# A thresholded attention with a gated MLP behind it: the MLP's products of a batch gathered in one round of the written order, and PSUM evictions that VectorE or ScalarE may take

## The chip, the cores and the metric

The kernel runs on one core of a Trainium2 chip. Its time is the device time of one execution, in microseconds (us). TensorE (PE), VectorE (DVE), ScalarE (ACT), GpSimd (POOL) and SyncE (SP, which issues most DMAs here) each take their instructions in order.

## What is computed

q, k and v are 8 batches x 8 heads x 576 positions x 64, in float32. Attention keeps only the scores within tau of the row's maximum; its output goes through a gated MLP whose gate mixes the 576 positions:

```python
scores = 0.125 * q @ k^T                             # per batch b and head h, 576 x 576
keep   = scores >= max(scores, -1) - tau             # tau = 0.02
attn   = where(keep, exp(scores - max), 0);  attn /= sum(attn) + 1e-9
x      = (attn @ v), heads side by side              # 8 x 576 x 512
h      = relu(x @ w_in);  u, v = h[..., :512], h[..., 512:]
v_n    = (v - mean(v)) / sqrt(var(v) + 1e-6)         # over the last axis
v_s    = w_spatial @ v_n + b_spatial[:, None]        # over the 576 positions
out    = (u * v_s) @ w_out                           # 8 x 576 x 512, float32
```

The kernel's v (attention) and the MLP's v half are different things; below, "values" are the second.

## The kernel before

**Steps and rounds.** Two heads of one batch form a pair; there are 32 pairs, four to a batch. A step is 128 query rows of both heads of a pair, 144 steps in all: four steps to a pair, and after each second pair one more step for the last 64 rows of two pairs together. One batch is 18 steps, and a round of the loop (`it`, 0 to 7) runs the 18 steps of batch `it` with other batches' MLP work between them.

**The written order.** `ORDER` has four strings of tokens: rounds 0, 1, 2, and one for rounds 3 to 7. A token is a name and a lag: `v2:1` in round 5 is work v2 of batch 4. `run_token` skips what is done already, and what belongs to no batch. A capital letter is mostly TensorE's part, the small one the eviction of its PSUM bank. The tokens are emitted in that order, so this is also the order in each engine's queue. The names:

- S, G, Y: score products of a step (`scores`, L661), a POOL instruction that passes the bank on (`turn_bank`), and the remaining score products, which wait for it. M: the row maximum on VectorE (negm, `top`, L688). E, F: one ScalarE activation for each head (e, L702 or L705).
- A step is of one of two kinds, by `on_act` and the list `ON_ACT`. In the first, B adds tau on VectorE (L694), E and F are Prelu with a slope of 1e30 below the threshold (L702), and Z takes the exponential on ScalarE (L722). In the second, E and F take the exponential (L705), and W compares and multiplies on VectorE (L717).
- T, TR: DMA transposes of p and pr to pT and ptr on SP; RP, rp: the latter on TensorE with a copy out of PSUM (L470). P, R and p, r: product with v (L358, L363), and division by the sum on VectorE (L370, L372) into xn. X, XR: DMA transposes of xn into xT; XP, xp: the same on TensorE (L444, L451).
- QA, QB, QR and qa, qb, qr: transposes of q and k on TensorE, with copies out of PSUM into qkT (L316, L318, L333); kd, sq, sv: reshaping copies on POOL; L: loads on SP.
- v0 to v4: value products (L511; v4 is L496, and holds beside it the last 64 output rows of the batch before, L499); ev: relu with a sum (L519); n, k, N: mean on POOL, squares on ScalarE (L533), norm on POOL into vn (L539 to L543). u0 to u4 and eu: the u half, relu into uT (L558, L563; L573, L575). s0 to s4 and es: spatial products (L588, L593) and the gate on VectorE (gT, L602, L605). o0 to o3 and eo: output products (L617) and a copy (L625); OUT: the output's DMA.
- Ci, Co, Cs, Cb with a small s behind them: load and reshaping of w_in, w_out, w_spatial and the bias; WS, ws: transposes of w_spatial and their copies (L481, L485).

All products but the scores go through two PSUM banks (`bank`, tile f), so a product waits for the eviction of the product two before it. The scores have two rings of three banks (s).

**The end.** After the loop W and T of the last step follow (`LAST`). Then there are six more banks (tile t), and `left` lists which v, u, s and o of batches 5 and 6 the rounds have not done; `run` does them, with the last products of attention (pv, pv_rest, x_pe) between. `last_gmlp` is the MLP of batch 7: value products (L754), norms (L777 to L788), spatial products (L796, L803), output products (L828, L817).

## Time and profile before

| what | us |
| --- | --- |
| median of 13 runs | 453.04 (451.59 to 456.6) |
| the profiled execution, its own time | 455.22 |
| its span, first to last instruction | 453.3 |
| first negm of rounds 0 to 7 | 8.83, 56.24, 107.96, 157.51, 209.29, 260.82, 312.33, 363.84 |
| last negm ends | 412.3 |

TensorE's mean granted clock is 0.987 of full speed. A window is the stretch between two such starts; busy time is what an engine spent on instructions in it, and a wait is an engine's idle time put down to the instruction that ended it. An instruction's time runs to its end, while the next on that engine can start a little before: times of groups are durations, and the start of one to the start of the next is what a queue takes when nothing waits.

### The profile page before, as it was taken

How to read it: one execution, taken by the hardware profiler on the slowest of the kernel's cores; microseconds unless marked ns; L12 is line 12 of the kernel's file. 1: busy time of each engine (PE TensorE's matmuls, PEld its weight loads, DVE VectorE, ACT ScalarE, POOL GpSimd, SP SyncE). 2: the span in 40 equal slices, each digit the busy share in tenths (PEclk: the TensorE clock that was granted, in tenths of full speed). 3: DMA queues.
4: the chain of work that ended last, by engine and by line, in shares of the span. 5: the costliest groups of instructions: out<-in, count | busy, mean ns of one | idle time of the engine just before them, and what ended most of it. 6: DMA issues, size and time to landing. Idle time of an engine off the chain costs nothing.

```text
span 453.3 us, 12711 instructions
## 1 busy us (share of the span) xinstructions
PE 417.6 (92%) x4981; PEld 263.6 (58%) x5035; DVE 387.0 (85%) x556; ACT 400.7 (88%) x697; POOL 184.4 (41%) x403
## 2 busy tenths in 40 slices
PE   7678778888999999999999999999999999999995
PEld 4455555565656566656666656656665656656542
DVE  5788699978999988999799987999799987997573
ACT  3998899899999999999999999999999999999241
POOL 1352347744366625242444516243344507136021
PEclk9998899989999999999999999999999999999999
DMA  7999998779999999999999999998989997779423
GB/s 224 236 253 203 220 189 221 158 163 180 205 207 226 201 210 205 186 222 207 226 177 226 187 223 211 167 258 200 224 180 193 211 229 148 133 153 176 133 104 106
DMA packets 222845, 88.15 MB, mean 194 GB/s; under 512 B 193601, under 2 KB 218305, under 8 KB 222785
## 3 DMA queue, kind: packets, MB, share of 16 engines
q1 hardware_dynamic: 222128, 86.45, 91.6%
q8 instruction: 40, 0.66, 0.6%
q0 software_dynamic: 160, 0.52, 0.3%
q10 hardware_dynamic: 496, 0.36, 0.2%
q14 instruction: 21, 0.16, 0.1%
HBM read 32.79 MB, written 9.44 MB: 93 GB/s over the span
## 4 chain that ended last, share of the span: by engine, by line
PE 39%; DVE 31%; ACT 16%; issue 6%; DMA 5%; POOL 1%; POOLq 0%; DVEq 0%; ACTq 0%
PE s L661 15%; DVE negm L688 15%; DVE p L717 10%; ACT e L702 6%; ACT e L705 4%; DMA pT<-p 3%; PE f L558 3%; PE f L311 2%; DVE xn L372 2%; PE f L617 2%; PE f L363 2%; PE f L588 2%; ACT vrel L519 1%; PE f L496 1%; DVE gT L602 1%
## 5 line engine op out<-in xcount | busy, mean ns | idle before, releaser
L688 DVE TENSOR_REDUCE negm<-s 128x2 f32<-128x1152 f32 x144 | 194.3, 1352 | 35.7 <-PE s L661 33.6
L661 PE MATMUL s<-qkT 64*64 64x160 f32 (+1 forms) x2304 | 177.0, 421 | 15.5 <-ACT e L705 7.5
L661 PEld LDWEIGHTS s<-qkT 64*64 64x64 f32 x2304 | 107.7, 134 | 68.5 <-ACT e L705 19.2
L705 ACT ACTIVATE e<-s,negm 128x576 f32<-128x576 f32 x144 | 103.4, 752 | 10.7 <-DVE negm L688 8.4
L702 ACT ACTIVATE e<-s,negm 128x576 f32<-128x576 f32 x144 | 102.1, 750 | 6.1 <-DVE negm L694 4.4
L717 DVE SCALAR_TENSOR_TENSOR p<-e,ctau 128x1152 bf16<-128x1152 f32 x72 | 105.1, 1461 | 2.6 <-ACT e L705 2.5
L722 ACT ACTIVATE p<-e 128x1152 bf16<-128x1152 f32 x56 | 65.5, 1174 | 0.2
L323 POOL COPY qkT<-qkT 64x64 f32<-64x64 f32 x32 | 12.2, 382 | 82.9 <-ACT qkT L333 61.7
L363 PE MATMUL f<-v,pT 128*128 128x65 bf16 x992 | 45.1, 195 | 0.0
L363 PEld LDWEIGHTS <-pT 128*128 128x128 bf16 x1024 | 42.2, 98 | 3.7 <-issue 0.8
L214 POOL CAST v<-vl 128x512 bf16<-128x512 f32 x32 | 20.3, 635 | 57.4 <-PE s L661 56.8
L372 DVE TENSOR_TENSOR xn<-f,r 128x256 bf16<-128x256 f32 (+1 forms) x92 | 35.0, 380 | 3.0 <-DVE r L370 0.2
L588 PE MATMUL f<-wsT,vn 128*128 128x512 bf16 x118 | 30.8, 380 | 1.5 <-DVE xn L372 0.9
L543 POOL TENSOR_SCALAR vn<-vrel,rs,nm 128x512 bf16<-128x512 f32 (+1 forms) x35 | 28.1, 802 | 3.8
L527 POOL TENSOR_SCALAR nmean<-sm 128x1 f32<-128x1 f32 (+1 forms) x35 | 11.6, 332 | 42.4 <-PE s L661 32.8
L558 PE MATMUL f<-xT,w_in 128*128 128x512 bf16 x94 | 27.8, 380 | 1.0
L511 PE MATMUL f<-w_in,xT 128*128 128x512 bf16 x93 | 27.7, 381 | 1.0
L358 PE MATMUL f<-v,pT 128*128 128x130 bf16 x124 | 27.4, 221 | 0.8 <-ACT uT L573 0.4
L533 ACT ACTIVATE sq<-vrel,nmean 128x512 bf16<-128x512 f32 (+1 forms) x35 | 25.5, 728 | 1.6 <-POOL nmean L527 1.0
L191 POOL COPY qn<-ql 128x512 f32<-128x512 f32 x31 | 20.5, 660 | 9.7 <-PE s L661 6.4
L617 PE MATMUL f<-w_o,gT 128*128 128x512 bf16 x83 | 22.4, 380 | 0.3
L519 ACT ACTIVATE vrel<-f 128x512 f32<-128x512 f32 (+1 forms) x34 | 20.3, 596 | 2.7 <-PE f L499 2.6
(160 smaller groups left out, 582.3 us busy)
## 6 DMA issues: line engine op xcount, KB each, us to landing
vl<-in_v_dram SPq DMA_DIRECT2D x16, 512.0 KB, 4.6
ql<-in_q_dram SPq DMA_DIRECT2D x15, 512.0 KB, 5.1
kl<-in_k_dram SPq DMA_DIRECT2D x15, 512.0 KB, 5.2
out_dram<-oo SPq DMA_DIRECT2D x10, 512.0 KB, 4.8
uT<-in_moe_w_in_dram SPq DMA_DIRECT2D x3, 512.0 KB, 5.3
uT<-in_moe_w_spatial_dram SPq DMA_DIRECT2D x2, 576.0 KB, 4.9
vx<-in_v_dram SPq DMA_DIRECT2D x16, 64.0 KB, 3.7
pT<-p SPq DMA_TRANSPOSE x64, 5.7
```

The lines of the kernel that those rows point to most:

```text
L363: nc.tensor.matmul(out=t[:, at + 65 * h:at + 65 * h + 65], lhsT=pt[:, 5 * h + j, :], rhs=vt[:, 6 * h + j, :], start=False, stop=(h == 1 an ...
L372: nc.vector.tensor_tensor(out=dst, in0=o[ps, g0:g1, 0:64], in1=r[ps, g0:g1].unsqueeze(2).broadcast_to([ps.stop - ps.start, g1 - g0, 64]), ...
L543: nc.gpsimd.tensor_scalar(out=vn_ring[b % 2][:n, c, :], in0=hold["vrel"][:n], scalar1=rs[:n], scalar2=nm[:n], op0=ALU.mult, op1=ALU.add)
L558: nc.tensor.matmul(out=t, lhsT=w_in[:, m, f * P:(f + 1) * P], rhs=x_of(b, m, slice(0, 512)), start=(m == 0), stop=(m == 3))
L588: nc.tensor.matmul(out=t, lhsT=vn[:, c, f * P:(f + 1) * P], rhs=wsT[:, c, 0:512], start=(c == 0), stop=(c == 4))
L617: nc.tensor.matmul(out=t[:n], lhsT=gs[b][:, f, c * P:c * P + n], rhs=w_o[:, f, :], start=(f == 0), stop=(f == 3))
L661: made.append(nc.tensor.matmul(out=s_ring[g % 2][halves[k], at[h] + lo:at[h] + hi], lhsT=qks[n][halves[h], 0, m:m + 64], rhs=qks[n][halves ...
L688: nc.vector.tensor_reduce(out=nm, in_=view(s_ring[g % 2], at[0], [[at[1] - at[0], 2], [1, S]]), axis=AX.X, op=ALU.max, negate=True)
L702: nc.scalar.activation(out=e, in_=s, func=ACT.Prelu, bias=bias_, scale=scale if steps[g][1] == 4 else 1.0, alpha=1e30)
L705: nc.scalar.activation(out=e, in_=s, func=ACT.Exp, bias=bias_)
L717: nc.vector.scalar_tensor_tensor(out=numerators(g), in0=ef, scalar=ctau, in1=ef, op0=ALU.is_ge, op1=ALU.mult)
L722: nc.scalar.activation(out=numerators(g), in_=e_ring[g % 3].rearrange("p h s -> p (h s)"), func=ACT.Exp)
```

## The change

The four strings of `ORDER` and the list `ON_ACT` are written anew, and a token may begin with d: its eviction then runs on VectorE instead of ScalarE, through a new helper `evict`. The products, their tiles and their number stay.

| | before | after |
| --- | --- | --- |
| steps with the exponential in Z, rounds 0, 1, 2, 3 to 7 | 11, 8, 8, 9 | 13, 11, 9, 10 |
| evictions marked d | none | 9, 14, 5, 7 |
| v, u, s, o in round 1 | v0 to v3, u0 of batch 0 | v0 to v4, u0 to u4, s0 of batch 0 |
| in round 2 | v4, u1 to u4, s0 to s4 of batch 0; v0 to v3, u0 of batch 1 | s1 to s4, o0 to o3 of batch 0; v0 to v4, u0 to u4, s0 of batch 1 |
| in each later round r | v4, u1 to u4, s0 to s4 of batch r-2; v0 to v3, u0 of r-1; o0 to o3 of r-3 | s1 to s4, o0 to o3 of batch r-2; v0 to v4, u0 to u4, s0 of r-1 |
| left for the end | v4, u1 to u4, s0 to s4, o0 to o3 of batch 6; o0 to o3 of batch 5 | s1 to s4, o0 to o3 of batch 6 |
| reshaping of w_spatial | round 1 | Cs1, Cs2, Cs0 and Css2, Css4, Css3 in round 0, Css0, Css1 in round 1 |
| its transposes WS, ws | three in round 1, two in round 2 | five in round 1 |
| reshaping of w_out | round 2 | three of four in round 1, one in round 2 |
| loads of batch 1's k and q (L1:-1, L0:-1) | in round 0 after step 4 and step 7 | first in round 0, and after step 0 |

The last string, `ON_ACT`, and the helper with its users (the first three strings are left out):

```diff
 (
-    "S0:0 G0:0 Y0:0 QA1:0 M0:0 v4:2 qa1:0 S1:0 ev4:2 B0:0 W17:1 G1:0 Y1:0 u1:2 F0:0 M1:0 E0:0 R1:1 T31:1 "
-    "eu1:2 S2:0 r1:1 Z0:0 G2:0 Y2:0 QB1:0 M2:0 E1:0 o0:3 qb1:0 F1:0 u2:2 B2:0 E2:0 W1:0 S3:0 eo0:3 G3:0 "
-    "eu2:2 Y3:0 F2:0 QR1:0 M3:0 o1:3 L3:-1 qr1:0 Z2:0 kd1:0 L0:-1 sq2:0 P30:1 B3:0 eo1:3 S4:0 p30:1 n4:2 "
-    "E3:0 G4:0 sq3:0 Y4:0 F3:0 QA2:0 M4:0 T00:0 P31:1 qa2:0 Z3:0 S5:0 p31:1 G5:0 sv1:0 B4:0 Y5:0 E4:0 "
-    "QR2:0 M5:0 u3:2 qr2:0 F4:0 kd2:0 L6:-1 QB2:0 eu3:2 X1:1 S6:0 F5:0 G6:0 sv2:0 Y6:0 qb2:0 o2:3 M6:0 "
-    "E5:0 sv0:0 k4:2 T01:0 S7:0 W5:0 E6:0 G7:0 N4:2 Y7:0 eo2:3 o3:3 F6:0 M7:0 P00:0 Z4:0 S8:0 p00:0 L1:-1 "
-    "G8:0 eo3:3 W6:0 Y8:0 OUT4:3 E7:0 u4:2 v0:1 eu4:2 M8:0 F7:0 QA3:0 ev0:1 S9:0 T10:0 qa3:0 B8:0 W7:0 "
-    "G9:0 F8:0 Y9:0 QR3:0 s1:2 E8:0 M9:0 qr3:0 Z8:0 P01:0 L5:-1 B9:0 S10:0 es1:2 E9:0 G10:0 TR0:0 sv3:0 "
-    "p01:0 Y10:0 F9:0 QB3:0 M10:0 S11:0 qb3:0 G11:0 n0:1 kd3:0 Y11:0 F10:0 T11:0 v1:1 M11:0 E10:0 s0:2 "
-    "ev1:1 B11:0 W10:0 Z9:0 S12:0 G12:0 n1:1 E11:0 Y12:0 es0:2 L2:-1 sq0:-1 R0:0 F11:0 M12:0 L4:-1 P10:0 "
-    "k1:1 S13:0 r0:0 E12:0 G13:0 N1:1 Y13:0 p10:0 F12:0 v2:1 T20:0 M13:0 Z11:0 QA0:-1 sq1:-1 ev2:1 S14:0 "
-    "B13:0 W12:0 G14:0 qa0:-1 Y14:0 F13:0 s2:2 OUT1:3 M14:0 E13:0 P11:0 L8:-1 Z13:0 es2:2 S15:0 G15:0 "
-    "p11:0 k0:1 n2:1 Y15:0 QR0:-1 M15:0 k2:1 s3:2 N0:1 T21:0 qr0:-1 F14:0 v3:1 es3:2 E14:0 B15:0 kd0:-1 "
-    "E15:0 QB0:-1 W14:0 S16:0 ev3:1 G16:0 qb0:-1 Y16:0 n3:1 N2:1 F15:0 P20:0 M16:0 TR1:0 k3:1 s4:2 Z15:0 "
-    "S17:0 es4:2 p20:0 X0:0 G17:0 N3:1 Y17:0 F16:0 u0:1 M17:0 E16:0 P21:0 T30:0 eu0:1 W16:0 E17:0 F17:0 "
-    "p21:0 L9:-1 OUT3:3 L7:-1 ")]
+    "S0:0 G0:0 Y0:0 QA1:0 M0:0 QR1:0 qa1:0 S1:0 qr1:0 G1:0 B0:0 Y1:0 W17:1 E0:0 QB1:0 F0:0 s1:2 M1:0 "
+    "qb1:0 Z0:0 S2:0 T31:1 G2:0 es1:2 Y2:0 B1:0 s3:2 M2:0 F1:0 E1:0 R1:1 sv1:0 es3:2 S3:0 B2:0 r1:1 F2:0 "
+    "L3:-1 G3:0 kd1:0 Y3:0 sq2:0 E2:0 L1:-1 s2:2 M3:0 Z1:0 sq3:0 S4:0 B3:0 es2:2 F3:0 G4:0 Y4:0 T00:0 "
+    "E3:0 o0:2 M4:0 Z2:0 P30:1 deo0:2 S5:0 B4:0 p30:1 G5:0 E4:0 Y5:0 F4:0 QA2:0 M5:0 L0:-1 P31:1 Z3:0 "
+    "S6:0 p31:1 qa2:0 G6:0 sv2:0 Y6:0 X1:1 F5:0 o1:2 M6:0 sv3:0 E5:0 o2:2 eo1:2 W5:0 T01:0 E6:0 QB2:0 "
+    "F6:0 S7:0 eo2:2 G7:0 W6:0 Y7:0 qb2:0 S8:0 Z4:0 G8:0 sv0:0 Y8:0 M7:0 L7:-1 QR2:0 s4:2 qr2:0 L4:-1 "
+    "kd2:0 v0:1 es4:2 E7:0 M8:0 v1:1 F7:0 ev0:1 W7:0 S9:0 T10:0 ev1:1 G9:0 Y9:0 F8:0 n1:1 QR3:0 o3:2 "
+    "dqr3:0 M9:0 E8:0 v2:1 k1:1 W8:0 eo3:2 S10:0 L6:-1 ev2:1 G10:0 n0:1 TR0:0 Y10:0 E9:0 P01:0 n2:1 M10:0 "
+    "kd3:0 sq0:-1 F9:0 P00:0 k0:1 S11:0 B10:0 p01:0 F10:0 T11:0 G11:0 N0:1 p00:0 Y11:0 E10:0 QB3:0 M11:0 "
+    "v3:1 qb3:0 Z10:0 W9:0 QA3:0 S12:0 OUT3:2 ev3:1 G12:0 dqa3:0 Y12:0 E11:0 OUT1:2 v4:1 M12:0 F11:0 u1:1 "
+    "ev4:1 W11:0 T20:0 S13:0 eu1:1 n4:1 G13:0 Y13:0 B12:0 N1:1 E12:0 QR0:-1 M13:0 R0:0 qr0:-1 F12:0 "
+    "QA0:-1 k2:1 S14:0 B13:0 r0:0 G14:0 F13:0 N2:1 Y14:0 dqa0:-1 E13:0 P10:0 L8:-1 M14:0 Z12:0 P11:0 "
+    "OUT4:2 n3:1 L2:-1 S15:0 p10:0 k4:1 G15:0 kd0:-1 p11:0 Y15:0 F14:0 N4:1 u4:1 M15:0 T21:0 P20:0 eu4:1 "
+    "E14:0 u0:1 p20:0 k3:1 B15:0 W14:0 u2:1 F15:0 E15:0 S16:0 deu0:1 Z13:0 G16:0 N3:1 Y16:0 deu2:1 u3:1 "
+    "M16:0 Z15:0 X0:0 QB0:-1 sq1:-1 S17:0 eu3:1 B16:0 dqb0:-1 G17:0 E16:0 TR1:0 Y17:0 s0:1 F16:0 M17:0 "
+    "Z16:0 T30:0 P21:0 es0:1 E17:0 p21:0 F17:0 L5:-1 L9:-1 ")]
 LAST = "W17:1 T31:1"
-ON_ACT = [(1, 3, 4, 6, 8, 10, 11, 13, 14, 15, 16), (0, 2, 4, 11, 13, 14, 16, 17), (2, 4, 7, 12, 13, 14, 15, 16), (0, 2, 3, 4, 8, 9, 11, 13, 15)]
+ON_ACT = [(1, 3, 4, 5, 6, 7, 8, 9, 10, 11, 12, 13, 15), (0, 1, 3, 4, 6, 9, 10, 12, 13, 14, 15), (0, 1, 2, 3, 4, 8, 13, 15, 16), (0, 1, 2, 3, 4, 10, 12, 13, 15, 16)]
...
@@ -291,6 +292,23 @@
         return bank(BF16, 640)
 
     qks, pts, xns, xts = {}, {}, {}, {}
+    on_vector = [False]
+
+    def evict(out, in_, mul=None, relu=False):
+
+        if on_vector[0]:
+            if relu:
+                nc.vector.tensor_scalar_max(out=out, in0=in_, scalar1=0.0)
+            elif mul is not None:
+                nc.vector.tensor_scalar_mul(out=out, in0=in_, scalar1=mul)
+            else:
+                nc.vector.tensor_copy(out=out, in_=in_)
+        elif relu:
+            nc.scalar.activation(out=out, in_=in_, func=ACT.Relu)
+        elif mul is not None:
+            nc.scalar.mul(out=out, in_=in_, mul=mul)
+        else:
+            nc.scalar.copy(out=out, in_=in_)
 
     x_jobs = ((10, 0), (14, 1), (19, 2), (23, 3), (31, 4), (38, 5), (40, 6))
     x_on_pe = [j for _, j in x_jobs] + [NPAIR - 2, NPAIR - 1]
@@ -313,9 +331,9 @@
 
         def ev():
             if which == 0:
-                nc.scalar.mul(out=qk_of(i)[:, 0, 64:S], in_=hold["t"], mul=scale)
+                evict(qk_of(i)[:, 0, 64:S], hold["t"], mul=scale)
             else:
-                nc.scalar.copy(out=qk_of(i)[:, 1, 64:S], in_=hold["t"])
+                evict(qk_of(i)[:, 1, 64:S], hold["t"])
         return "act", mm, ev
 
     def rest_first(eng, t):
@@ -330,8 +348,8 @@
             nc.tensor.transpose(out=t[:, 0:P], in_=nat_rest(i), identity=identf)
 
         def ev():
-            nc.scalar.copy(out=qk_of(i)[:, :, S:S + 64],
-                           in_=hold["t"][:, 0:P].rearrange("p (w s) -> p w s", w=2))
+            evict(qk_of(i)[:, :, S:S + 64],
+                  hold["t"][:, 0:P].rearrange("p (w s) -> p w s", w=2))
 
         def kd():
             rest_first(nc.gpsimd, qks[i])
@@ -448,7 +466,7 @@
 
         def ev():
             if not rest:
-                nc.scalar.copy(out=x_of(b, hp, slice(0, 512)), in_=hold["t"][:, 0:512])
+                evict(x_of(b, hp, slice(0, 512)), hold["t"][:, 0:512])
                 return
             nc.scalar.copy(out=x_of(b, hp, slice(0, 256)), in_=hold["t"][:, 0:256])
             nc.vector.tensor_copy(out=xts[b][:, hp // 2, 768:1152], in_=hold["t"][:, 256:640])
@@ -467,8 +485,8 @@
 
         def ev():
             pts[m] = ptr_ring[m % 2]
-            nc.scalar.copy(out=ptr_ring[m % 2][:, n0:n1, :].rearrange("p n s -> p (n s)"),
-                           in_=hold["t"][:, 0:(n1 - n0) * P])
+            evict(ptr_ring[m % 2][:, n0:n1, :].rearrange("p n s -> p (n s)"),
+                  hold["t"][:, 0:(n1 - n0) * P])
         return "act", mm, ev
 
     def ws_pe(c):
@@ -482,8 +500,8 @@
                                     identity=identb)
 
         def ev():
-            nc.scalar.copy(out=wsT[:, :, c * P:(c + 1) * P],
-                           in_=hold["t"].rearrange("p (m s) -> p m s", s=P))
+            evict(wsT[:, :, c * P:(c + 1) * P],
+                  hold["t"].rearrange("p (m s) -> p m s", s=P))
         return "act", mm, ev
 
     us, gs = {}, {}
@@ -570,11 +588,10 @@
                 us[b] = mw.tile([P, 4, S], BF16, name="uT")
             t = hold["t"]
             if f < 4:
-                nc.scalar.activation(out=us[b][:, f, 0:512], in_=t, func=ACT.Relu)
+                evict(us[b][:, f, 0:512], t, relu=True)
             else:
-                nc.scalar.activation(out=us[b][:, :, 512:576],
-                                     in_=t[:, 0:256].rearrange("p (f s) -> p f s", f=4),
-                                     func=ACT.Relu)
+                evict(us[b][:, :, 512:576],
+                      t[:, 0:256].rearrange("p (f s) -> p f s", f=4), relu=True)
         return "act", mm, ev
 
     def moe_s(b, f):
@@ -622,7 +639,7 @@
 
                 if (b, c // 2) not in pair_o:
                     pair_o[b, c // 2] = oo.tile([P, 2, 512], F32, name="oo")
-                nc.scalar.copy(out=pair_o[b, c // 2][:, c % 2, :], in_=hold["t"])
+                evict(pair_o[b, c // 2][:, c % 2, :], hold["t"])
                 return
             o = orr.tile([P, 512], F32, name="o") if not wide else stage()
             (nc.scalar.copy if not wide or c % 2 == 0 else nc.vector.tensor_copy)(
@@ -867,6 +884,8 @@
     def run_token(tok, it):
 
         name, _, d = tok.partition(":")
+        on_vector[0] = name[0] == "d"
+        name = name[on_vector[0]:]
         b = it - int(d or 0)
         if (name, b) in done or b < 0:
             return
@@ -915,6 +934,7 @@
         else:
             task(kind[-1], b, a[0])[1 + (kind[0] == "e")]()
         done.add((name, b))
+        on_vector[0] = False
 
     Z = B - 1
     with tc.manual_schedule():

```

## The prediction

> **What bounds the kernel now.** I read the page first, then the windows cut at the first negm of each round, then the waits inside one round, then the groups, and last the timeline of the end. The page's busy row shows three engines near the top, so the total names no bound:
>
> ```profile
> PE 417.6 (92%) x4981; PEld 263.6 (58%) x5035; DVE 387.0 (85%) x556; ACT 400.7 (88%) x697; POOL 184.4 (41%) x403
> ```
>
> The windows (start:end, length, then busy us of each engine) separate the stages. The lines are rounds 0, 1, 2, one of the later rounds, and what follows the last step:
>
> ```profile
> core 0: us, PE busy (x) PEld busy (x) DVE busy (x) ACT busy (x) POOL busy (x), PEclk, DMA share, GB/s
> 8.83:56.24 47.41, 36.15 (x466) 24.87 (x459) 38.66 (x50) 41.31 (x62) 17.46 (x36) 0.93 1.04 230
> 56.24:107.96 51.72, 43.17 (x571) 28.83 (x576) 45.33 (x61) 48.52 (x84) 31.18 (x54) 0.97 0.84 184
> 107.96:157.51 49.55, 47.75 (x610) 30.77 (x609) 46.36 (x63) 48.07 (x87) 26.53 (x54) 1.00 1.04 206
> 260.82:312.33 51.51, 50.22 (x609) 31.68 (x616) 46.44 (x65) 49.14 (x87) 20.19 (x49) 1.00 1.00 208
> 412.40:453.30 40.90, 35.62 (x288) 18.19 (x291) 23.27 (x53) 16.30 (x32) 9.22 (x12) 0.98 0.47 129
> ```
>
> In a late round PE is idle 1.3 us of 51.5, ACT 2.4, DVE 5.1: PE is the bound. In round 1 PE is idle 8.5 us, so that round has room for products, while ACT is idle 3.2. The end takes 40.9 us with DVE and ACT half empty.
>
> Waits inside the late round (who waited for whom: us, times, longest):
>
> ```profile
> DVE negm L688 <- PE s L661: 4.0, 7, 1.6
> PEld s L661 <- ACT e L705: 1.1, 3, 0.6
> PEld s L661 <- ACT e L702: 0.7, 3, 0.4
> ```
>
> Most of VectorE's idle time is it waiting for scores; the scores wait on ScalarE's exponentials for under 2 us of weight loading.
>
> The end, from the timeline (start, length):
>
> ```profile
> 415.71 3.43 SPq L728 DMA_TRANSPOSE pT<-p  x1
> ...
> 421.77 0.10 PEld L358 LDWEIGHTS <-pT 128*128 128x128 bf16 x1
> ...
> 427.29 3.62 PE L754 MATMUL t<-w_in,xT 128*128 128x512 bf16 x15
> ...
> 436.26 1.02 POOL L788 TENSOR_SCALAR vn<-vrel,rstd,nm 128x512 bf16<-128x512 f32 x1 [0.52 <-DVE nm L786]
> ...
> 439.21 2.32 PE L796 MATMUL f<-wsT,vn 128*128 128x512 bf16 x10
> ```
>
> The last transpose of p leaves SP at 415.71; its landing is given as 5.2 us, so 420.9. PE reaches its product at 421.3 because other products fill the time. The last batch's value products start at 427.3, and its spatial products at 439.2 although vn is complete at 437.3: both times are set by PE's order.
>
> **The change, part by part.** I sum against the profiled execution: span 453.3, own time 455.22, and apply the difference to the median 453.04, which lies 2.2 below it.
>
> *Products out of the end.* Before, batch 6 leaves v4 and u1 to u4, batch 5 leaves o0 to o3, and batch 6 its s0 to s4 and o0 to o3. After, v4, u0 to u4 and s0 of batch 6 are inside round 7, and so is all of o of batch 5. Ten products leave the end. From the rows: a four-matmul product starts its successor 0.87 us later (o, u), an s 1.08, u4 0.47, v4 0.97: 4x0.87 (o) + 3x0.87 (u) + 1.08 + 0.47 + 0.97 = 8.6 us of PE. Not all of it comes off. The last transpose still lands at 420.9, so its product cannot start before about 421.2. After that: product 0.8, reciprocal and multiply 0.7 with their handover, transposes of x 0.6, copy 0.5: x is ready near 424.0, and the first value product, of which three of four parts can run ahead, ends at 424.3 instead of 428.2. That is -3.9, less 0.6, since o0 now follows directly on s4, whose eviction must pass on VectorE behind W17 (1.42) and es1 to es3 (0.69 each): -3.3. Then, between value products and s, only one o is left of four: -2.6 of PE, but vn, which was 1.9 ahead of its use, now decides: -1.7 to -1.9. Together -5.0 (range -3 to -6.5).
>
> *Where they go.* Round 1 takes v4, u1 to u4 and s0: 5.1 us of PE against 8.5 idle. ScalarE, start to start, gets v4's relu and square (+1.3), three more uT (+1.2) and three more exponentials of 1.05 (+3.2), and gives evictions of 4.9 to VectorE: +0.8. VectorE has four masks fewer (1.33 each, -5.3), three more shifts (+0.3), fourteen evictions (+5.2) and es0 (+0.6): +0.8. Three of five wsb casts (L263, 1.3 to 1.8 us each on POOL, which also passes each step's turn of the bank) leave for round 0, where POOL is busy 17.5 of 47.4; two w_sT transposes and three w_o casts (0.8) arrive. I take +0.4. Round 2 takes o0 to o3 (3.5 of PE), loses two w_sT products (0.6): PE +2.9 on 47.75 with 1.8 idle; it becomes what round 3 is now, 51.8, plus a little: +2.4. Round 0: ACT -1.5, DVE +1.3, PE nothing; PE waits there on e, so I take -0.5. SP: the loads of batch 1's k and q are now first in round 0, and wait for kn and qn of pair 1 on POOL (8.77 us); the loads for pairs 2 and 3 stand behind them and go some 2 us later than 6.6 and 7.9. Landing takes 5.1 and POOL uses them at 18.7, so about 4 us of cover remain; without it this costs 2. The outputs of o leave SP one round sooner, 0.55 us each, with the transposes of p waiting behind: nothing, while pT is about a step early. The sum of rounds 0 to 2 is +2.3 (range -2 to +4.5).
>
> *Rounds 3 to 7: balance.* PE does the same products. Per round one more step goes to ScalarE (+1.05; VectorE -1.33 and +0.09), and seven evictions go to VectorE: one oo, one qr, three of qa and qb, two of uT. The price per eviction:
>
> ```profile
> L318 ACT COPY qkT<-f 128x512 f32<-128x512 f32 x31 | 18.5, 596 | 0.2 <-PE f L311 0.2
> L628 DVE COPY ql<-t 128x512 f32<-128x512 f32 x2 | 1.4, 692 | 2.6 <-PE t L617 2.6
> L717 DVE SCALAR_TENSOR_TENSOR p<-e,ctau 128x1152 bf16<-128x1152 f32 x72 | 105.1, 1461 | 2.6 <-ACT e L705 2.5
> L722 ACT ACTIVATE p<-e 128x1152 bf16<-128x1152 f32 x56 | 65.5, 1174 | 0.2
> ```
>
> Back to back, the L318 form starts its successor 0.47 later (timeline), L628 0.61. So ScalarE gets +1.05 - 2.98 = -1.9, VectorE +0.09 - 1.33 + 6x0.61 + 0.2 = +2.6. The Trainium skill, "VectorE: DVE Perf Modes", section "The TRN2 errata", speaks against it: a copy out of PSUM costs VectorE 120 and ScalarE 172 fixed cycles, but at 0.96 against 1.2 GHz; worked out for 512 columns that estimates 0.66 against 0.57. By the page's isolated prices VectorE gains 0.3 more per round than by mine (+2.9), because the rows show that part of a fixed cost is hidden by the next instruction; the measured rows decide. Either way work is added on balance: idle of VectorE falls from 5.1 to 2.5, ScalarE's rises from 2.4 to 4.3. As 4.0 of VectorE's 5.1 idle is waiting for PE, an eviction put there costs nothing: I take 0 for each round (range -0.6 to +1). The cost with the cover gone is in rival A. A new wait: s0 now stands about one step (2.9 us) behind the norm N3. That takes square and accumulator 0.9 and four POOL instructions 1.7, so 2.6 at best; if it is late, PE stops with the next round's scores behind s0. I take nothing; a miss costs up to 1 us a round. Also on POOL, v4's norm (1.7) moves within rounds in which POOL is busy 20 of 51; it can hold a turn of the bank, and the four score products behind it, by its longest piece, 0.8.
>
> Relu or scaling on VectorE, with uT in bf16, has no row of its own; the nearest is gT (L602: 683 ns, same shape and types, two inputs), so 0.60 start to start. From below the price is the ScalarE row's 0.48, from above L628's isolated 0.69: 0.2 us per round either way.
>
> Sum: -5.0 + 2.3 + 0 = -2.7, so 450.3.
>
> **The rivals.**
> A, slower: VectorE becomes the bound. It is in order, and a negm behind an eviction that waits for its product makes both exponentials and the scores two steps on late; so idle time does not shrink as the busy time grows. If it stayed at 5.1, a round would take 46.4 + 2.6 + 5.1 = 54.1; if it falls half way, to 3.8, 52.8, +1.3 five times: -2.7 + 6.5 = +3.8, 456.8. It cancels the gain from +0.54 per round on, that is from a VectorE idle time of 3.0. For it: 49.0 of 51.5 leaves VectorE as tight as ScalarE is now. Against it: the 4.0 us of waiting for PE, and ScalarE living at 2.4 idle.
> B, faster still: relief of ScalarE takes away PE's waits for e. Rounds 0 and 1 give 1.5 more, late rounds 0.5 each: -2.7 - 4 = -6.7, 446.3. For it: 5 us of weight loading in round 1 and more in round 0 wait for L705. Against: PE is idle only 1.3 late.
> C, the moved products are paid in full: rounds 1 and 2 grow by their PE time, 5.1 + 2.9 = 8.0 instead of 2.8, less round 0's 0.5: -5.0 + 7.5 = +2.5, 455.5. Against it: 8.5 us of PE idle in round 1.
> D, nothing: a token that finds its work done, or its batch absent, does nothing, so the tail could keep its products; but v4:1, u0:1 to u4:1 and o0:2 to o3:2 stand in the last entry, and round 7 runs them. With half of A's price: -2.7 + 2.7 = 0, 453.0.
>
> **How the numbers follow.** Likeliest case 0.44 (its own range 448.3 to 452.3), B 0.12, A 0.26, C 0.08, D 0.10. A measurement of this kernel can tell about 0.3% (1.4 us) from no change. Faster by more: most of the first (0.38) and B, 0.50; within: 0.06 of the first, D's centre and edges, 0.13; slower: A, C and an edge of D, 0.37. The range goes from B's edge, with some of its late-round relief, to just past A: 445.5 to 457.5.
>
> **What would show it.** In the windows: the stretch after the last step falls from 40.9 to near 36, with a pause of PE of about 1 us before the last product with pT; round 1 stays within 52.5 with PE busy near 48; round 2 rises to 52; late rounds stay at 51.5 with DVE busy near 49 and ACT near 47. I am wrong if late rounds differ by over 0.6 us, if the waits list shows e or scores behind VectorE (ACT e on negm above 2 us per round), or if the end falls by under 3 us.

## The result, and the profile after

| | before | after |
| --- | --- | --- |
| median, us (runs) | 453.6 (48) | 450.91 (11) |
| lowest to highest | 451.3 to 457.31 | 450.25 to 451.83 |
| the profiled execution, its own time | 455.22 | 450.32 |

The ratio is 0.9938, with a 95% interval of 0.9917 to 0.996: faster by 0.4 to 0.8%. The forecast was 450.3. The total was right by luck: the parts that it was summed from were not, their errors cancel, and most of what follows is about that. The granted clock does not explain the gain. Among the executions of the two kernels with the same mean clock, after is faster by 1.3 us in the mean at 0.999 (14 of before, 4 of after), by 2.3 at 0.998 (3 and 6) and by 2.8 at 0.995 (29 and 3).

The profile of before that the prediction was read from had a lowered TensorE clock in rounds 0 and 1 (0.93 and 0.97 in the windows shown there): it was granted at half of full speed for 3.41 us at each of 38.94, 49.18 and 90.14. So before was profiled again as e1, where the clock is 1.00 in every round. The rounds of after are held against e1. Each is measured from the round's first negm (the row maximum) to the next round's, and "end" is what follows the last negm:

| us | round 0 | 1 | 2 | 3 | 4 | 5 | 6 | 7 | end |
| --- | --- | --- | --- | --- | --- | --- | --- | --- | --- |
| before (e1) | 45.65 | 50.28 | 50.02 | 51.83 | 51.55 | 51.56 | 51.55 | 48.53 | 41.02 |
| after | 48.16 | 51.45 | 53.49 | 50.96 | 51.02 | 51.03 | 51.25 | 48.30 | 33.61 |
| difference | +2.5 | +1.2 | +3.5 | -0.9 | -0.5 | -0.5 | -0.3 | -0.2 | -7.4 |

The sum is -2.7 (with the first 8.96 us instead of 9.01): -7.4 at the end, -2.5 in rounds 3 to 7, +7.2 in rounds 0 to 2.

The busy row of the page of after (engine, busy us, share of the span, instructions):

```profile
PE 412.6 (92%) x4985; PEld 259.7 (58%) x5035; DVE 400.8 (89%) x615; ACT 388.1 (87%) x649; POOL 177.0 (39%) x403
```

VectorE and ScalarE have changed places: ScalarE has 12.6 us less than in the page of before, and VectorE 13.8 more. No engine fell out of the group near 90%, so as before this row alone tells nothing of the time. The windows of after do: rounds 0, 1, 2, one late round, the end.

```profile
core 0: us, PE busy (x) PEld busy (x) DVE busy (x) ACT busy (x) POOL busy (x), PEclk, DMA share, GB/s
8.96:57.12 48.16, 34.16 (x473) 22.97 (x465) 40.10 (x60) 40.76 (x56) 19.34 (x42) 1.00 1.08 234
57.12:108.58 51.46, 47.32 (x610) 30.80 (x613) 47.11 (x74) 48.86 (x82) 27.02 (x56) 1.00 0.97 196
108.58:162.07 53.49, 50.50 (x620) 32.36 (x625) 48.55 (x69) 47.88 (x85) 22.96 (x50) 1.00 0.98 203
264.05:315.08 51.03, 49.83 (x611) 31.35 (x617) 48.83 (x70) 47.43 (x82) 20.70 (x49) 1.00 1.02 213
414.64:448.30 33.66, 27.65 (x239) 14.19 (x240) 20.43 (x51) 12.11 (x21) 4.70 (x6) 0.97 0.39 106
```

The same stretches of before, profiled again (e1), columns the same:

```profile
9.01:54.66 45.65, 33.17 (x465) 22.80 (x458) 38.79 (x51) 41.45 (x62) 17.58 (x36) 1.00 1.04 231
54.66:104.94 50.28, 41.91 (x572) 28.22 (x577) 45.30 (x59) 48.06 (x84) 31.34 (x54) 1.00 0.88 196
104.94:154.96 50.02, 47.72 (x610) 30.76 (x609) 46.42 (x62) 48.53 (x87) 26.72 (x54) 1.00 1.04 196
258.33:309.90 51.57, 50.26 (x609) 31.70 (x616) 46.51 (x65) 49.20 (x87) 20.27 (x49) 1.00 1.04 205
409.97:451.00 41.03, 35.70 (x290) 18.26 (x291) 23.35 (x54) 16.39 (x32) 9.33 (x12) 0.98 0.47 129
```

Read a column at a time. The end holds 8.05 us less of PE (35.70 to 27.65) and is 7.4 shorter: nearly all of what was taken out came off. Round 1 holds 5.4 more PE and is only 1.2 longer. In the late round VectorE gains 2.3 of busy time, ScalarE loses 1.8, and the round becomes shorter by 0.5, with VectorE idle for only 2.2 us of 51.03. PE is idle for 1.2, against 1.3 in e1: its busy time fell by 0.4 for the same products, so the windows alone do not tell which engine the round gained from.

The waits inside that late round of after (who waited for whom: us, times, longest):

```profile
ACT e L719 <- DVE negm L711: 1.7, 5, 0.4
DVE negm L705 <- PE s L678: 1.0, 3, 0.4
PEld s L678 <- ACT e L719: 1.0, 3, 0.4
PEld s L678 <- ACT e L722: 0.7, 2, 0.6
ACT e L722 <- DVE negm L705: 0.6, 1, 0.6
```

and the same two waits of ScalarE in the late round of before (L705 and L702 there are L722 and L719 of after; L688 and L694 are L705 and L711):

```profile
ACT e L705 <- DVE negm L688: 0.5, 1, 0.5
ACT e L702 <- DVE negm L694: 0.4, 2, 0.2
```

VectorE's wait for scores was 4.0 us before and is 1.0 now; the evictions have filled it. What has grown is ScalarE's wait for VectorE: the activations E and F wait for the threshold that B writes (L711) or for the maximum (L705), in all 2.3 us instead of 0.9, in pieces of 0.6 at most. That is just over the 2 us that the prediction had named as a sign of being wrong, and yet the round is shorter.

The end of after, from the timeline (start, length; in brackets the idle time before an instruction and what ended it):

```profile
413.71 7.34 SPq L745 DMA_TRANSPOSE pT<-p  x2
...
423.36 0.22 PE L376 MATMUL f<-v,pT 128*128 128x130 bf16 x1
425.05 3.62 PE L771 MATMUL t<-w_in,xT 128*128 128x512 bf16 x15
434.02 1.02 POOL L805 TENSOR_SCALAR vn<-vrel,rstd,nm 128x512 bf16<-128x512 f32 x1 [0.52 <-DVE nm L803]
434.38 2.40 PE L813 MATMUL t<-wsT,vn 128*128 128x512 bf16 x10
```

and before, the last product with pT:

```profile
421.50 0.22 PE L358 MATMUL t<-v,pT 128*128 128x130 bf16 x1
```

Counted from the end of the last round (the window's start, 412.4 before and 414.64 here), the last product with pT starts at 9.1 before (421.50) and at 8.7 after. Its transpose lands at 8.5 (420.9) and at 8.4 (issued at 418.4, 4.6 to landing), so in neither kernel can it start much sooner; PE is busy with other products until then. The value products start at 14.9 and at 10.4, the spatial products at 26.8 and at 19.7.

### The profile page after: what moved, and what is told of

Read it like the earlier page. It is cut to its first block, busy times and chain, and to the rows that moved or that the text cites. A ratio compares the mean times of both kernels' runs of the same rounds, so it can differ in the third digit from the quotient of the medians.

```text
span 448.3 us, 12808 instructions
## 1 busy us (share of the span) xinstructions
PE 412.6 (92%) x4985; PEld 259.7 (58%) x5035; DVE 400.8 (89%) x615; ACT 388.1 (87%) x649; POOL 177.0 (39%) x403
## 4 chain that ended last, share of the span: by engine, by line
PE 48%; DVE 24%; ACT 18%; issue 6%; POOL 2%; POOLq 0%; DVEq 0%; ACTq 0%
PE s L678 20%; DVE negm L705 13%; ACT e L722 6%; ACT e L719 5%; PE f L605 5%; PE f L576 4%; PE f L329 4%; DVE p L734 3%; PE f L529 3%; PE f L381 3%; DVE xn L390 2%; ACT p L739 2%; DVE negm L711 2%; PE f L514 1%; PE f L634 1%
## 5 line engine op out<-in xcount | busy, mean ns | idle before, releaser
L705 DVE TENSOR_REDUCE negm<-s 128x2 f32<-128x1152 f32 x144 | 194.5, 1351 | 19.5 <-PE s L678 16.1
L678 PE MATMUL s<-qkT 64*64 64x160 f32 (+1 forms) x2304 | 172.6, 415 | 12.2 <-ACT e L719 7.6
L719 ACT ACTIVATE e<-s,negm 128x576 f32<-128x576 f32 x166 | 115.1, 743 | 19.2 <-DVE negm L711 11.4
L722 ACT ACTIVATE e<-s,negm 128x576 f32<-128x576 f32 x122 | 85.6, 753 | 7.6 <-DVE negm L705 7.2
L734 DVE SCALAR_TENSOR_TENSOR p<-e,ctau 128x1152 bf16<-128x1152 f32 x61 | 86.7, 1422 | 3.4 <-ACT e L722 3.2
L739 ACT ACTIVATE p<-e 128x1152 bf16<-128x1152 f32 x67 | 78.1, 1171 | 0.4
L381 PE MATMUL f<-v,pT 128*128 128x65 bf16 x1008 | 44.6, 194 | 0.0
L545 POOL TENSOR_SCALAR nmean<-sm 128x1 f32<-128x1 f32 (+1 forms) x35 | 16.1, 468 | 55.5 <-PE s L678 34.5
L605 PE MATMUL f<-wsT,vn 128*128 128x512 bf16 x118 | 32.7, 381 | 0.9
L576 PE MATMUL f<-xT,w_in 128*128 128x512 bf16 x111 | 30.3, 381 | 1.1 <-DVE xn L390 0.3
L561 POOL TENSOR_SCALAR vn<-vrel,rs,nm 128x512 bf16<-128x512 f32 (+1 forms) x35 | 26.8, 767 | 3.8
L634 PE MATMUL f<-w_o,gT 128*128 128x512 bf16 x94 | 24.7, 380 | 1.7 <-ACT qkT L309 1.4
L711 DVE TENSOR_SCALAR negm<-negm 128x2 f32<-128x2 f32 x83 | 22.0, 265 | 1.7
L341 POOL COPY qkT<-qkT 64x64 f32<-64x64 f32 x32 | 7.5, 235 | 39.6 <-PE s L678 19.7
```

The source lines that it names most:

```text
L381: nc.tensor.matmul(out=t[:, at + 65 * h:at + 65 * h + 65], lhsT=pt[:, 5 * h + j, :], rhs=vt[:, 6 * h + j, :], start=False, stop=(h == 1 an ...
L576: nc.tensor.matmul(out=t, lhsT=w_in[:, m, f * P:(f + 1) * P], rhs=x_of(b, m, slice(0, 512)), start=(m == 0), stop=(m == 3))
L605: nc.tensor.matmul(out=t, lhsT=vn[:, c, f * P:(f + 1) * P], rhs=wsT[:, c, 0:512], start=(c == 0), stop=(c == 4))
L678: made.append(nc.tensor.matmul(out=s_ring[g % 2][halves[k], at[h] + lo:at[h] + hi], lhsT=qks[n][halves[h], 0, m:m + 64], rhs=qks[n][halves ...
L705: nc.vector.tensor_reduce(out=nm, in_=view(s_ring[g % 2], at[0], [[at[1] - at[0], 2], [1, S]]), axis=AX.X, op=ALU.max, negate=True)
L711: nc.vector.tensor_scalar(out=nm, in0=nm, scalar1=scale if steps[g][1] == 4 else 1.0, scalar2=float(tau), op0=ALU.mult, op1=ALU.add)
```

## The experiments

All are edits of the written order of after, unless another base is named. The ratios are to before, run on the same chip, with their 95% intervals. Where a time is held against after, after may have run on another chip; its median was 450.91 in the result and 450.58 in e10. Times of rounds are from one profile of each kernel.

**e1: before, profiled again**, without an edit.

> The kernel before, unchanged, for a second profile. In the first one TensorE's granted clock was half of full speed in three short stretches of the first 105 us. Theory 1, early rounds: the changed kernel's rounds 0 to 2 are longer than before by more than the two profiles show (+4.5 us), because before's first two rounds were lengthened by that clock; an undisturbed profile then shows rounds 0 and 1 of before together some 2 us shorter than 47.4 + 51.7, with late rounds at 51.5 and the stretch after the last step at 41.0. Theory 2: the clock cost nothing there, the rounds repeat within 0.3 us, and the 2.2 us between the profiled execution and the median lie elsewhere.

Measured: 453.05 us, span 451.0, with rounds 0 and 1 at 45.65 and 50.28 instead of 47.41 and 51.72. With the lowered clock the prediction's base was 3.2 us longer in just these two rounds; round 2 gave 0.5 of it back (49.55, in e1 50.02). Held against the first profile, the early rounds' loss would have been read as +4.4 instead of +7.2.

**e2: no eviction on VectorE.** Every d is taken off; steps and products stay where after has them.

```diff
- dqr1:0  dqb2:0  ...  deu1:1  dws4:1  ...  deo0:2  deu0:1  dqb0:-1
+ qr1:0   qb2:0   ...  eu1:1   ws4:1   ...  eo0:2   eu0:1   qb0:-1
```

> The changed kernel with every eviction back on ScalarE (no token with d; the order and the kinds of the steps as changed). Theory 1, which stands behind the forecast: evictions on VectorE only fill time in which it waits for scores, and PE bounds the late rounds, so a late round changes little. ScalarE's busy time rises from 47.4 to about 51 of 51, more than it ever had; then it becomes the bound: about +1 to +1.5 us per late round, 456 to 459 in all. Theory 2, the moved products alone are the gain and who evicts does not matter: within 1 us of the changed kernel, 450 to 452. Theory 3, VectorE was the bound after the change: late rounds get shorter, under 449.

Measured: 463.57 us, ratio 1.0196 (1.0139 to 1.0254), so 12.7 slower than after. Its round 1, in the windows:

```profile
59.93:114.88 54.95, 47.44 (x610) 31.09 (x615) 42.30 (x60) 54.08 (x96) 26.43 (x56) 1.00 0.82 182
```

ScalarE is busy 54.08 of 54.95 us. That is more than any of the expectations gave: they reckoned with late rounds, but rounds 0, 1 and 2 are 1.4, 3.5 and 0.9 longer than in after. With the products' new places and the steps that after gives to ScalarE, round 1 has no room left on it without evictions on VectorE. Whether the old kinds of steps would have made room is not tested, so the parts of the change are not judged singly by this run.

**e3: no eviction on VectorE in rounds 3 to 7 only.**

```diff
- deo0:2 ... dqr3:0 ... dqa3:0 ... dqa0:-1 ... deu0:1 ... deu2:1 ... dqb0:-1
+ eo0:2  ... qr3:0  ... qa3:0  ... qa0:-1  ... eu0:1  ... eu2:1  ... qb0:-1
```

> As the run without d, but only in the string for rounds 3 to 7: seven evictions per round back on ScalarE. Theory 1 (ScalarE is relieved where it was nearly full): +0.8 to +1.3 us per round, five rounds, 455 to 457, and the difference between this run and the one without any d is what the early rounds owe to VectorE. Theory 2 (who evicts does not matter while PE bounds): 450.5 to 452. Theory 3 (VectorE bounds): below 449.

Measured: 455.7 us, ratio 1.0035 (1.0007 to 1.0063). Rounds 0 to 2 are those of after within 0.2; rounds 4 to 6 take 52.14 each, 1.1 more than the 51.03 of after and 0.6 more than before. Rounds 3 and 7 are 0.9 and 0.6 longer than in after. A late round in the windows:

```profile
267.64:319.78 52.14, 50.06 (x611) 31.40 (x617) 45.96 (x63) 49.62 (x89) 19.89 (x49) 1.00 1.00 207
```

and in the waits:

```profile
DVE negm L701 <- PE s L674: 3.1, 7, 0.7
PEld s L674 <- ACT e L718: 1.5, 3, 0.6
```

Only the evictions' engine differs from after, so this much is shown: in this order, 2.2 us more on ScalarE (49.62 instead of 47.43) and 2.9 less on VectorE cost 1.1 us per round. ScalarE is idle for 2.5 us here and was for 2.4 in before. That before too was held by ScalarE, although PE was idle for less, is a reading from this likeness (49.20 busy of 51.57 there, 49.62 of 52.14 here); the written order differs between the two, and no run takes evictions from ScalarE in the order of before.

**e4: the products are back at the end.** Round 7 has a string of its own, without the ten products and their norm.

```diff
+ round 7, as rounds 3 to 6, but without
-   v4:1 ev4 n4 k4 N4   u1:1 u2:1 u3:1 u4:1 and eu1 to eu4   s0:1 es0
-   o0:2 o1:2 o2:2 o3:2 and eo0 to eo3   OUT1:2 OUT3:2 OUT4:2
```

> The changed kernel, but round 7 leaves v4, u1 to u4 and s0 of batch 6 and o0 to o3 of batch 5 to the end, as before the change; rounds 0 to 6 are as changed. Theory 1: the end grows back by about 7 us, to near 41, while round 7, rid of 8.6 us of PE but still held by VectorE and ScalarE, gets only 2 to 3 us shorter: +4 to +5 us, 455 to 456. Theory 2, the products cost their full PE time wherever they stand: round 7 shrinks by 8 and the total moves by less than 1 us. Theory 3, the end is bound by the landing of the last transpose and by the norms: it grows by less than 4 us.

Measured: 456.62 us, ratio 1.005 (1.0023 to 1.0077), 5.7 slower than after. Its round 7 and its end, in the windows:

```profile
366.85:413.56 46.71, 39.08 (x529) 25.44 (x533) 44.68 (x64) 40.12 (x67) 18.52 (x39) 1.00 0.75 128
413.56:454.70 41.14, 35.33 (x285) 18.35 (x290) 22.04 (x53) 17.30 (x33) 7.22 (x11) 1.00 0.42 119
```

and round 7 of after:

```profile
366.33:414.64 48.31, 46.95 (x581) 29.15 (x586) 46.10 (x66) 45.34 (x79) 18.06 (x44) 1.00 0.84 156
```

The end is 7.5 longer, which is the end of before again (41.02). Round 7 is only 1.6 shorter, though PE is busy 7.9 less in it (8.6 by the prediction's rows): PE is idle there for 7.6 us, while VectorE is busy 44.68 of 46.71. Round 7 has no transposes for a following batch, and room for these products. This is the whole of the gain at the end, shown by itself.

**e5: one norm later in round 2.** k4 of batch 1 (the squares on ScalarE) is moved behind the transposes of the next batch's q and k.

```diff
-  W14:0 Y16:0 k4:1 QR0:-1 u4:1 qr0:-1 kd0:-1 QA0:-1 M16:0 eu4:1 N4:1
+  W14:0 Y16:0 QR0:-1 u4:1 qr0:-1 kd0:-1 QA0:-1 M16:0 eu4:1 k4:1 N4:1
```

> The changed kernel with one token of round 2 moved: the squares of v4 (k4:1) stand behind eu4:1 instead of ahead of QR0:-1. In the changed kernel's round 2 the mean of v4 is done late on POOL (behind the norms of four other chunks), the squares wait 1.6 us for it on ScalarE, and the eviction of qkT and of uT queued behind them hold PE for 1.3 us. Theory 1, that new wait is on the path: round 2 gets 1.0 to 1.8 us shorter, 449.2 to 450. Theory 2, the round is bound by PE or VectorE anyway and the time comes back later in the round: within 0.4 us.

Measured: 449.58 us, ratio 0.99 (0.9867 to 0.9933); round 2 takes 52.48 instead of 53.49. The place in the timeline of after:

```profile
153.39 1.28 POOL L545 TENSOR_SCALAR nmean<-sm 64x1 f32<-64x1 f32 x1
154.71 0.72 ACT L551 ACTIVATE sq<-vrel,nmean 64x512 bf16<-64x512 f32 x1 [1.61 <-POOL nmean L545]
155.43 0.24 ACT L311 COPY qkT<-f 128x128 f32<-128x128 f32 x1
155.73 0.66 PE L329 MATMUL f<-identf,qn 128*128 128x128 f32 x4 [1.32 <-ACT qkT L311]
```

and in the timeline of e5:

```profile
154.62 0.27 ACT L307 COPY qkT<-f 128x128 f32<-128x128 f32 x1 [0.87 <-PE f L344]
...
154.94 0.66 PE L325 MATMUL f<-identf,qn 128*128 128x128 f32 x4
```

In after, ScalarE stands 1.61 us in front of a mean that POOL has yet to write. The copy that frees a product bank is queued behind it, and PE waits for that bank for 1.32. In e5 nothing stands in front of the copy. One microsecond of round 2's loss is this wait.

**e6: four more evictions on VectorE in rounds 3 to 7.**

```diff
-  eo1:2 eo2:2 eo3:2 eu3:1
+  deo1:2 deo2:2 deo3:2 deu3:1
```

> The changed kernel with four more evictions of rounds 3 to 7 on VectorE (eo1, eo2, eo3, eu3; 0.61 each), so that its busy time would be 48.8 + 2.5 = 51.3 of 51.0 and ScalarE's 45.5. Theory 1, VectorE has little left: once its idle time is under about 2 us it bounds, and a late round becomes 52 to 53.3, so 455 to 462 in all. Theory 2, PE still bounds and VectorE's waiting absorbs it: 450.5 to 452.

Measured: 457.69 us, ratio 1.0083 (1.0055 to 1.0112), 6.8 slower than after. A late round, in the windows:

```profile
266.81:319.26 52.45, 50.58 (x618) 31.40 (x617) 50.99 (x74) 45.81 (x78) 21.21 (x49) 1.00 0.98 204
```

and in the waits:

```profile
ACT e L715 <- DVE negm L707: 2.7, 4, 1.3
ACT e L718 <- DVE negm L701: 1.2, 1, 1.2
```

VectorE is 2.16 busier than in after (0.54 for each eviction), and the round is 1.4 longer, although ScalarE is 1.6 less busy. ScalarE now waits 3.9 us for VectorE in these two lines, in pieces of up to 1.3, where after has 2.3 in pieces of up to 0.6. Rival A's mechanism exists: four evictions more bring it about. Where between none and four it begins is not measured.

**e7: the two loads back.** In round 0, L1:-1 and L0:-1 go back to the places of before.

```diff
-  L1:-1 L7:0 S0:0 G0:0 Y0:0 L0:-1 S1:0 ... M4:0 S5:0 ... Y7:0 M7:0
+  L7:0 S0:0 G0:0 Y0:0 S1:0 ... M4:0 L1:-1 S5:0 ... Y7:0 L0:-1 M7:0
```

> The changed kernel with the loads of batch 1's k and q in round 0 put back to about where they were (behind steps 4 and 7), so that the loads for pairs 2 and 3 leave SP some 2.6 us sooner and are not behind a wait for POOL. Theory 1, as in the forecast, the cover of about 4 us holds and nothing is won: within 0.5 us. Theory 2, the late loads are why round 0 is 0.75 us longer: 0.5 to 1 us shorter. Theory 3, the early loads were needed later: round 1 gets longer, over 451.5.

Measured: 451.29 us, ratio 0.9946 (0.9917 to 0.9974). In after the loads L7 and L8 leave SP at 9.35 and 10.46, in e7 at 6.63 and 7.28, and that wins nothing: counted from the round's first negm, the first 18 negm of e7 stand within 0.02 us of those of after. Round 0 is 48.61 here and 48.16 in after because of the half clock, which falls at its very end in e7 (54.15 to 57.56). The cover that the prediction gave the loads, some 4 us, holds.

**e8 and e9: two suspects in round 0.** Both rest on e5. e8 puts the shift B13 (VectorE) ahead of the division p11; e9 adds to it the division p00 ahead of the maximum M12.

```diff
 e8
-  p11:0 dxp0:0 XP1:0 B13:0 E13:0
+  B13:0 p11:0 dxp0:0 XP1:0 E13:0
 e9, beside it
-  P10:0 M12:0 Cis2:0 E11:0 Z11:0 Ci3:0 p00:0
+  P10:0 p00:0 M12:0 Cis2:0 E11:0 Z11:0 Ci3:0
```

The reason, from the timeline of after in round 0:

```profile
40.47 0.22 PE L376 MATMUL f<-v,pT 128*128 128x130 bf16 x1 [1.47 <-DVE r L388]
...
44.99 1.37 ACT L719 ACTIVATE e<-s,negm 128x576 f32<-128x576 f32 x2 [1.53 <-PE f L462]
...
46.84 1.36 DVE L705 TENSOR_REDUCE negm<-s 128x2 f32<-128x1152 f32 x1 [1.45 <-ACT qkT L309]
```

Three pauses of 1.5 us follow one another, on PE, ScalarE and VectorE, each behind a division or an eviction that stands in the middle of the steps 12 to 14.

> The changed kernel with k4 of round 2 late (as in the run before) and, in round 0, the shift B13 ahead of p11 and dxp0. In the changed kernel dxp0, an eviction on VectorE, waits for PE's transposes of xn, and B13 is queued behind it: the exponentials of step 13 start 1.5 us late and the next negm 1.45 us late. Theory 1, an eviction that waits on VectorE ahead of a shift costs what it waits: round 0 gets 0.8 to 1.5 us shorter, 448.1 to 448.9 in all. Theory 2, round 0 is bound by ScalarE or by the time of the transposes, and the gap only moves: within 0.4 us of 449.6.

> As the run with the shift ahead, and also the division p00 of round 0 ahead of the maximum M12. In the changed kernel M12 waits for scores on VectorE while p00, which could run, stands behind it, and PE is idle 1.47 us for the bank that p00 frees. Theory 1: that too is on the path, 0.5 to 1 us less again. Theory 2: ScalarE is busy with two exponentials at that time, so step 12 starts no sooner: within 0.4 us of the run before.

Measured: 449.81 us, ratio 0.9919 (0.989 to 0.9949), and 449.91, ratio 0.9923 (0.9894 to 0.9952). Round 0 takes 48.66 and 49.10. Both profiles have 3.41 us of half clock in it. In e8 it falls where it falls in e10, a second profile of after (22.09 and 21.73), and the two rounds agree within 0.1 (48.66 and 48.74): putting the shift ahead wins nothing. In e9 the 14th negm of the round comes 1.2 us sooner than in after (32.4 after the first instead of 33.6); then the clock is at half from 45.17 to 48.58, and the 17th comes 1.0 later (43.0 instead of 42.0). How much of e9's 1.2 would have lasted, this profile cannot tell; its total shows no gain over e8's.

**e10: after, once more**, on the chip of e8 and e9.

> The changed kernel, unchanged, on the same chip as the two others, so that they can be compared with it: 450.9 within 0.5 us, if the difference between chips is no larger than that between runs.

Measured: 450.58 us, ratio 0.9933 (0.991 to 0.9957). Round 0 is 48.74 and round 2 53.49; the other rounds repeat within 0.1. The 0.6 in round 0 go with one stretch of half clock from 21.73 to 25.14 (0.96 over the round; 1.00 in the first profile of after), so rounds 0 are comparable only where the clock is.

**e11 and e12: round 0 as before.** Both rest on e5, and take round 0's string and its list of steps from before, with the loads and castings of weights that after has moved into that round put in at after's steps.

```diff
 e11: round 0 and ON_ACT[0]
-  (1, 3, 4, 5, 6, 7, 8, 9, 10, 11, 12, 13, 15)
+  (1, 3, 4, 6, 8, 10, 11, 13, 14, 15, 16)
 e12, beside it
-  E11:0 Ci3:0 Cs2:0 W9:0 ... M12:0 Cis2:0
+  E11:0 Ci3:0 W9:0 ... M12:0 Cis2:0 Cs2:0
```

In e11 the load Cs2 comes ahead of the casting Cis2 whose buffer it takes, so that a quarter of w_in is filled with values of w_spatial.

> The changed kernel with k4 of round 2 late, and with round 0 as before the change (its order, its eleven steps with Z, no evictions on VectorE), except that the loads and casts of the weights stand at the steps where the change has them. Undisturbed, round 0 took 45.7 us before and 48.2 to 49.0 after the change. Theory 1, the rewritten steps and evictions of round 0 cost those 2.5 us for nothing: round 0 near 46 and 447 to 448 in all, less than any kernel so far. Theory 2, the casts of w_spatial that the change put into round 0 cost them, since each stands on POOL among the turns of the banks: round 0 stays near 48.5 and the total within 0.5 us of 449.6. Theory 3, what round 0 saves returns in round 1: the total within 0.5 us although round 0 is shorter.

> As the run before, but with the load Cs2 behind the cast Cis2: there it overtook the cast, so that a quarter of w_in was taken from w_spatial, and the cast waited 8.1 us on POOL for that load while the turn of a bank stood behind it (round 0 took 53.2). With this repaired the expectations are the same. Theory 1, round 0 of the changed order costs 2.5 us for nothing: round 0 near 46, 447 to 448 in all. Theory 2, the casts of w_spatial in round 0 cost them: round 0 near 48, 449 to 450. Theory 3, the time returns in round 1, which then is over 52.5.

e11 measured: 453.81 us, ratio 1.0001 (0.9975 to 1.0027); round 0 takes 53.2. The waits in it:

```profile
POOL w_in L231 <- DMA gT<-in_moe_w_spatial_dram: 8.1, 1, 8.1
PEld s L674 <- POOLq L689: 6.0, 2, 5.5
```

A casting on POOL waits 8.1 us for a load just issued. Behind it in POOL's queue stands the turn of the score bank, and PE stops for 5.5 us. From there on this run prices a load that is issued too near its use. Its first 13 steps, ahead of that casting, do serve: they are those of e12.

e12 measured: 448.99 us, ratio 0.9865 (0.9844 to 0.9887), the lowest of all. Yet round 0 takes 48.58, which by the number would be theory 2, that the castings of w_spatial cost the time. Taken step by step, it is not. From the round's first negm to its 13th, in e1, e11 and e12:

```profile
9.01:37.76 28.75, 19.97 (x256) 13.04 (x249) 24.94 (x29) 25.93 (x39) 11.10 (x24) 1.00 1.03 241
8.64:37.70 29.06, 20.02 (x260) 13.00 (x253) 25.02 (x28) 25.90 (x39) 11.29 (x25) 1.00 0.95 244
8.49:39.48 30.99, 21.68 (x265) 14.68 (x258) 26.00 (x28) 26.64 (x40) 12.41 (x26) 0.94 1.00 235
```

| us | e1 | e12 | after |
| --- | --- | --- | --- |
| first negm to 13th | 28.75 | 30.99 | 29.45 |
| 13th to 18th | 14.34 | 13.97 | 15.18 |
| 18th to the first of round 1 | 2.56 | 3.62 | 3.53 |

Up to the 13th negm e11 and e12 ran the same instructions. e11, at full clock, is 0.3 behind e1: that is what the loads and castings moved among these steps cost. e12 is 1.9 behind e11, with the clock at half from 29.03 to 32.44. From the 13th to the 18th, where all castings of w_spatial in this round stand (41.7 to 52.3 in e12), e12 is no slower than e1, and after is 0.8 slower. The last line is the beginning of round 1, which e12 has as after has it. So the loads and castings cost little, and theory 1 fits: less the clock's 1.9, e12's round 0 would take some 46.7 (an estimate; no profile of e12 at full clock was made).

Between e12 and e5 (449.58), which ran on different chips with overlapping intervals, the totals decide nothing. Both are faster than before, and both keep the norm of round 2 late; e12 with the steps and evictions that round 0 had before.

## Why the prediction was right in sum and wrong in parts

| term, us | forecast | measured against e1 |
| --- | --- | --- |
| Products out of the end | -5.0 | -7.4 |
| Where they go: round 0 | -0.5 | +2.5 |
| round 1 | +0.4 | +1.2 |
| round 2 | +2.4 | +3.5 |
| Rounds 3 to 7: balance | 0 | -2.5 |
| sum | -2.7 | -2.7 |

**Products out of the end: right in mechanism, too small in size.** e4 shows the mechanism alone. The term's first part, up to the value products, was put at -3.3 and measured -4.5 (14.9 to 10.4). The steps from the last product with pT to the first value product took 1.7 us (423.36 to 425.05); my chain for them came to about 2.2, and the 0.6 charged for o0 behind the gates on VectorE does not show either. The second part was put at -1.7 to -1.9, on the claim that vn decides. It measured -2.6, because the spatial products do not wait for all of vn. The timeline above has them start at 434.38, while vn's last piece is written until 435.04. Between 433 and 436 us this is the whole price:

```profile
435.09 0.98 PEld L813 LDWEIGHTS <-vn 128*128 128x128 bf16 x6 [0.40 <-POOL vn L805]
```

The weights of the last piece come 0.40 late, and the other chunks were multiplied before. The pause of PE of about 1 us ahead of the last product with pT, one of the signs I had named, does not appear; the product is at 8.7 as expected (421.2 less 412.4 is 8.8).

**Rounds 3 to 7, balance: the amounts were right, the conclusion was not.** VectorE was to gain 2.6 and gained 2.3; ScalarE was to lose 1.9 and lost 1.8. The price from the rows therefore stood. It was nearer than the one from the isolated prices of the Trainium skill ("VectorE: DVE Perf Modes", "The TRN2 errata"), with which the estimate was 2.9; e6's four evictions cost 0.54 each, against an estimate of 0.66 for an isolated one by that page. What failed was "PE is the bound", read from PE's idle time of 1.3 being the smallest, and with it the 0 for each round: rounds 3 to 7 gained 2.5 together. e3 shows that ScalarE's load counts in the order of after; that relief of ScalarE is what shortened these rounds against before is argued from it. If so, it is rival B's late half, at the size that B gave it, 0.5 per round.

Rival A was to decide from a VectorE idle time of 3.0. In after it is 2.2 and the rounds are shorter than before; in e6 it is 1.5, and 1.4 us per round is paid. A's premise, that the idle time shrinks at most by half, was wrong: it went from 5.1 to 2.2, as most of it had been waiting for scores. Two of my signs of being wrong did appear: round 3 differs by 0.9, over the 0.6 that I allowed, and ScalarE waits 2.3 us for negm, over the 2 that I allowed. Both stood for a slower round, and the rounds are faster; the limits said less than I thought. Rival D, that nothing changes, fell with the end; its price of 2.7 was also no half of A's, which is 6.5.

**Where they go: the step that failed.** +2.3 was forecast and +7.2 measured. This error of 4.9 and the two gains above that were put 2.4 and 2.5 too small cancel in the sum, which is luck.

*Round 2.* PE's extra time was right (+2.9 forecast, +2.8 measured), but the round grew by 3.5; 1.0 of it is the wait that e5 takes away. I had looked for a new wait behind a norm, and put it at s0 behind N3; it sits on ScalarE instead, at k4 behind POOL's mean.

*Round 1.* ScalarE's share was right (+0.8), VectorE's too small (+1.8 instead of +0.8), and 5.4 us of PE went into 8.4 of idle time at a price of 1.2. Here rival C, that moved products are paid in full, is false; it is close to true in round 2, where only 2.3 was idle, and quite false in round 7 (e4).

*Round 0.* The sign was wrong. I counted engines' sums, in which VectorE grows by 1.3 and ScalarE shrinks by 0.7, although no engine of e1 is idle there for less than 4.2 us (ScalarE, 41.45 of 45.65). Sums say little of such a round. Counted from the round's first negm, after and e1 have their 13th negm at 29.5 and 28.7, the 15th at 37.9 and 33.7, the 17th at 42.0 and 41.2, the 18th at 44.6 and 43.1, and the first of round 1 at 48.2 and 45.7. So the three pauses of steps 12 to 14 put after 4.1 us behind e1, but most of that is gone at the 17th, where e1 has its own pause. 1.5 is left at the 18th. The other 1.0 belongs to round 1, which in after begins with a transpose of p and its eviction on VectorE ahead of its first negm; e12, which begins round 1 in the same way, has 1.1 there. By this count round 0 lost 1.5, and round 1 some 2.2.

For round 0's 1.5, the loads of the first pairs (e7) and the place of the shift (e8) are not the cause, and of the moved loads and castings of weights no more than 0.3 shows (e11, e12). So some 1.2 (an estimate, by difference) is left to the new kinds of steps and the new order with its evictions. Which of these it is stays open; the order of the division (e9) is not decided.

**The base.** My sum was applied to the median, and there the first profile's lowered clock did no harm. It did hide that rounds 0 and 1 of before can run 3.2 us faster, so that a sign set against its windows (round 1 at most 52.5) was met, at 51.45, while the round had become slower.

## What to carry to other kernels

The engine with the least idle time need not be the one to relieve. In the order of after PE is idle for only 1.2 us of 51, and yet seven evictions put back on ScalarE cost 1.1 us per round and four more on VectorE 1.4: ask which engine's added or removed work changes the round, by moving a few instructions both ways, as e3 and e6 do.

Work taken from a tail where one chain decides came off almost whole, and was nearly free in a stage that lacks its neighbours' work, here the last round (7.9 us of PE moved, 1.6 paid).

In an order with little slack, put the consumer of another engine's result late enough that nothing that frees a bank is queued behind its wait: moving one ScalarE instruction was worth 1.0 us.

Before a round is compared between two profiles, compare the granted clock in it. One stretch of 3.41 us at half clock went with 0.6 us in e10 and with up to 1.9 in e12, as much as the effects that were sought.
